# The first dense matrix in seven products: a change to an attention, experts and dense kernel

## The chip, the cores and the metric

The kernel is one program on one core of a Trainium2 chip. The metric is the device time of one execution in microseconds, as the median of several runs. Five engines work side by side and are tied by semaphores only: PE multiplies matrices into PSUM, whose eight banks hold 512 float32 columns each on 128 partitions; DVE and ACT do elementwise work and empty PSUM; POOL issues the indirect transfers and does a little elementwise work; SP issues the other transfers. Each engine takes its instructions strictly in the order of the program, so an instruction that waits holds back all that stands behind it on its engine.

## The reference, cut to what matters

```python
def reference(q, k, v, moe_w_gate, moe_w1, moe_w2, moe2_w_in, moe2_w_out):
    x = retention(q, k, v)              # per head: (q k^T / 8 * decay) v; 4608 tokens x 512
    logits = x @ moe_w_gate             # 8 experts
    e = argmax(logits); gate = softmax(logits)[e]
    y = gate * (max(x @ w1[e], 0) @ w2[e])      # 512 -> 1024 -> 512, one expert per token
    h = y @ moe2_w_in                   # 512 -> 2048
    r = max(h, 0); g = r * r
    return g @ moe2_w_out               # 2048 -> 512
```

The gate is positive and the last two layers are a square and a matrix after it, so a gate on the rows of y is the same as its square on the rows of the output.

## The kernel before

Precision first, since it sets the count of the matmuls: every operand is held as a high part (`F32R`) and the rest (`lo`), and a product is three matmuls, high·high, high·low, low·high.

The program has three stages. **Attention** takes 36 tiles of 128 tokens and writes x to `x_d` in DRAM. **The experts** run in a loop over 64 units `u` (expert `e = u // 8`, slice `f = u % 8` of 128 hidden features). A unit multiplies 640 gathered tokens: `first(u + 1)` is 24 matmuls of 320 columns in two halves, each into one of three banks `l1_ps`; ACT writes the high part `hh` and DVE the rest `hl` of each half (L718, L719), after which the bank is free; `second(u)` is 15 matmuls of 512 columns (L736 to L738). So PE takes `first(u + 1)` before `second(u)`, and the second half of the next unit's `first` wants the bank of this unit's first half. Beside that a unit splits the weights of a later unit (`split_unit`, L97 and L98, on DVE, for one unit in eight on POOL), turns the next expert's tokens (`transp`, L684 to L689, for f of 2 to 6) and, for 32 of the units, changes 512 columns of the dense weights, which come as the two 32-bit words of a float64, into a high and a low part (`split_wide`, L119 to L147: seven DVE operations, two on ACT), which SP writes to `wd_d` in DRAM. At u = 18 stands `rest_of` (L757 on, the branch at L759), a branch (`tc.If`) for tokens beyond an expert's 640 places; with this input it is not taken, but every engine passes it. The last six units hold back their `second`, which then runs token tile by token tile, so that `finish` (gate times accumulator, scattered to `y_d`) frees the first rows early.

**The dense stage** has 9 blocks of 512 tokens and 16 slices of 128 hidden features. All 16 slices of both weight matrices stay on the chip as 16 tiles of 1 MB (pools `w_a`, `w_b`, `w_c`, `w_d`), loaded once. `up(b, f)` (L937) is 12 matmuls of 512 columns, `squares` is relu on ACT, square on DVE, high part on ACT and rest on DVE, `down(b, f)` (L958 to L960) 12 matmuls into four accumulator banks. For the first block the first four slices run in halves of 256 columns, since the rows of its last two tiles arrive late. The order is written by hand: `up` runs two steps ahead of `down`, and block b + 1 is fetched from `y_d` and turned during block b.

Of the kernel before, what the change touches and what calls it, by code (L numbers as in the profile page):

```python
# [19 lines left out]
NT = 36  # L20
# [7 lines left out]
REST = 18  # L28
# [3 lines left out]
GROUPS = [(0, 8), (8, 16), (16, 24), (24, 30), (30, 36)]  # L32

# [4 lines left out]
def body(ctx, tc, att, tab_v, tab_x, masks, wg, ident, pick, cst, wu, wd, out):  # L38
# [9 lines left out]
    w_a = scope(ctx, "w_a", 4)  # L48
    pools = {}
    early = ctx.enter_context(ExitStack())  # L50
    places = scope(early, "places", 1, side="right")
# [4 lines left out]
    wd_d = dram.tile([NF, 128, 2, 1024], F32, name="wd_d")  # L56
    x_d = dram.tile([NTOK, 512], F32, name="x_d")
    l_d = dram.tile([NTOK, NE], F32, name="l_d")
# [3 lines left out]
    cf = const.tile([128, C_N], F32, name="cf")  # L62
    ub = places.tile([128, 128], BF16, name="ub")
    sel = places.tile([128, 4, 128], F32, name="sel")
    ones = places.tile([128, 128], BF16, name="ones")
    rk = places.tile([128, NT], I32, name="rk")
    inv = places.tile([128, 2 * NS], F32, name="inv")
# [22 lines left out]
    def load_unit(u, on=None):  # L90
        raw = (on or pools["stg"]).tile([128, 1024], F32, tag="raw", name="raw")
        sp.dma_start(out=raw, in_=wu[u])
        return raw

    def split_unit(u, raw, on):
        w = ring(u).tile([128, 2, 1024], F32R, tag="w", name="w")
        act.activation(out=w[:, 0], in_=raw, func=AF.Copy)  # L97
        on.tensor_tensor(out=w[:, 1], in0=raw, in1=w[:, 0].bitcast(F32), op=ALU.subtract)  # L98
        return w
# [11 lines left out]
    def load_wide(j):  # L111
        raw = pools["cr_p"].tile([128, 512, 2], I32, tag="craw", name="craw")
        v, s = divmod(j, 2)
# [5 lines left out]
    def split_wide(j, raw):  # L119
        v, s = divmod(j, 2)  # L120
        low, high = raw[:, :, 0], raw[:, :, 1]
        m = pools["cv_p"].tile([128, 512], F32, tag="cm", name="cm")
        x = pools["cv_p"].tile([128, 512], F32, tag="cx", name="cx")
        t = pools["cv_p"].tile([128, 512], I32, tag="ct", name="ct")
        a = pools["cv_p"].tile([128, 512], F32, tag="ca", name="ca")
# [9 lines left out]
            out=a.bitcast(I32), in0=xi, scalar=-0x40000000, in1=t, op0=ALU.bitwise_and, op1=ALU.bitwise_or  # L135
        )
        vec.tensor_scalar(
            out=m.bitcast(I32), in0=a.bitcast(I32), scalar1=-0x800000, scalar2=None, op0=ALU.bitwise_and
        )
        vec.scalar_tensor_tensor(  # L140
            out=x, in0=low.bitcast(U32), scalar=2.0 ** -52, in1=m, op0=ALU.mult, op1=ALU.mult
        )
        w = pools["cw_p"].tile([128, 2, 512], F32R, tag="cw", name="cw")
        act.activation(out=w[:, 0], in_=a, func=AF.Copy)
        vec.tensor_tensor(out=a, in0=a, in1=w[:, 0].bitcast(F32), op=ALU.subtract)
        vec.tensor_tensor(out=w[:, 1], in0=a, in1=x, op=ALU.add)
        return lambda: sp.dma_start(out=wd_d[v, :, :, 512 * s:512 * s + 512], in_=w.bitcast(F32))  # L147

    def load_dense(v, wpool):
        w = wpool.tile([128, 2, 1024], F32R, tag="w", name="w")  # L150
        sp.dma_start(out=w.bitcast(F32), in_=wd_d[v])
        w_q[NE * 8 + v] = w
# [57 lines left out]
    def fetch_logits(sm, index, n):  # L210
        lg = sm.tile([128, n, NE], F32, tag="lg", name="glg")
        for i in range(n):
            fetch_rows(lg[:, i], l_d[:, :], index[:, i:i + 1])
        return lg

# [17 lines left out]
    def gate_of(sm, lg, n):  # L233
        mx = sm.tile([128, n], F32, tag="mx", name="gmx")
        vec.tensor_reduce(out=mx, in_=lg, axis=AX.X, op=ALU.max)
        vec.tensor_tensor(out=lg, in0=lg, in1=mx.unsqueeze(2).to_broadcast([128, n, NE]), op=ALU.subtract)
        act.activation(out=lg, in_=lg, func=AF.Exp)
        vec.tensor_reduce(out=mx, in_=lg, axis=AX.X, op=ALU.add)
        vec.tensor_scalar(out=mx, in0=mx, scalar1=1e-9, scalar2=None, op0=ALU.add)
        g = sm.tile([128, n], F32, tag="g", name="gg")  # L240
        vec.reciprocal(out=g, in_=mx)
        return g

    w_q = {}

# [6 lines left out]
    with ExitStack() as es:  # L252
# [14 lines left out]
        lgt = rt.tile([128, NT, NE], F32, name="lgt")  # L267
# [143 lines left out]
        def group(t0, t1):  # L411
# [3 lines left out]
            def one():  # L415
                lg = lgt[:, t0:t1]
                late.append(
                    lambda: sp.dma_start(
                        out=l_d[128 * t0:128 * t1, :].rearrange("(t p) e -> p t e", p=128), in_=lg
                    )  # L420
                )
# [84 lines left out]
        def lead_rows():  # L506
# [5 lines left out]
            for i in range(LEAD):  # L512
                row = pools["cv_p"].tile([128, 512], F32, tag=("cm", "cx")[i], name="lead")
                fetch_rows(row, x_d[0:128 * GROUPS[2][1], :], lead_idx[:, i:i + 1])
                lead_s.append(row)

        def lead_turn(i):
            ps = sc_ps.tile([128, 4, 128], F32, tag="sc", name="turn")
            turn_rows(ps, lead_s[i])
# [5 lines left out]
        raw = {}  # L525
        lead_x = [
            pools["cw_p"].tile([128, 2, 512], F32R, tag="cw", name=f"lead{s}").rearrange(
                "p s (k n) -> p (s k) n", n=128 * LEAD
            ) for s in range(2)
# [30 lines left out]
        for t in range(NT):  # L560
# [39 lines left out]
            if t % 6 == 2 and 12 <= t < 36:  # L600
                w_q[t // 6 - 2] = split_unit(t // 6 - 2, raw.pop(t - 2), pool)
# [4 lines left out]
        for v, tags in ((4, ("ct", "ca")), (5, ("cm", "cx"))):  # L606
            halves[v] = [pools["cv_p"].tile([128, 512], F32, tag=t, name="half") for t in tags]
# [4 lines left out]
    pools["w_b"] = scope(ctx, "w_b", 4, reuse="tile")  # L612
    xs_p = scope(ctx, "xs_p", 1, reuse="tile")
    xf_p = scope(ctx, "xf_p", 2, reuse="tile")
# [3 lines left out]
    yi, yt = {}, {}  # L618
# [4 lines left out]


    def fetch(b, t0=0, t1=4):
        if t0 == 0:
            yi[b] = xs_p.tile([128, CT, 4, 128], F32, tag="xs", name="yi")
            yt[b] = columns()
        y = yi[b].rearrange("q t a c -> q (t a) c")
        rows = y_d[512 * b:512 * b + 512, :].rearrange("(t i) (a c) -> a i t c", i=32, a=4)  # L630
        ts = slice(4 * t0, 4 * t1)
        for a in range(4):
            d = sp.dma_start(out=y[32 * a:32 * a + 32, ts], in_=rows[a][:, ts])  # L633
            if b < 2:
# [6 lines left out]
            if b == 0:  # L641
                read.append(d.ins)

    def turn(b, *tiles, chunks=(slice(0, 4),)):
        src = {i: xf_p.tile([128, 4, 128], F32, tag="xf", name="yf") for i in tiles}
        for ks in chunks:
            for i in tiles:
                vec.transpose(
                    out=src[i][:, ks].rearrange("f k (t i) -> f k t i", i=32),
                    in_=yi[b][:, i].rearrange("q t (k j) -> q k t j", k=4)[:, ks],  # L650
                )
        for ks in chunks:
# [438 lines left out]
```

## Time and profile before

| | |
|---|---|
| median of 3 runs | 1433.29 us (1427.59 to 1435.78) |
| the profiled execution | 1436.04 us, of which the span from first to last instruction 1434.2 us |
| PE busy | 1391.3 us (97%) |
| DVE, ACT, POOL busy | 712.5 us (50%), 435.3 us (30%), 313.2 us (22%) |
| granted PE clock, mean | 0.991 of full speed |
| moved by DMA | 172.51 MB, mean 120 GB/s |

Busy is the time in which at least one instruction of the engine ran, so overlapping matmuls count once. The stages, by the slices of the page: attention to about 200 us, experts to 644 us, dense to the end.

### The profile page before, as it was taken

Reading aid. Unit: us, or ns where it says so; the run is one execution under the profiler, and the core shown is the slowest. Engines: PE = TensorE matmul, PEld = TensorE weight load, DVE = VectorE, ACT = ScalarE, POOL = GpSimd, SP = SyncE. Lnnn points to the kernel's source line nnn. Section 1 sums busy time; section 2 is a strip of 40 time slices with the busy share of each in tenths; the row PEclk is TensorE's granted clock in tenths of the full one; section 3 lists DMA queues with packets and bytes.
Section 4 is the critical chain, followed back from the end, with each engine's and each line's share of the span. In section 5 each row is a group of like instructions: output and inputs, shape, how many; then the busy total and the mean of one; then the engine's idle time right before and its main releaser. Section 6 shows DMA issues by size and latency. Waiting matters only on the chain.

```text
span 1434.2 us, 20323 instructions
## 1 busy us (share of the span) xinstructions
PE 1391.3 (97%) x8217; PEld 1192.2 (83%) x8217; DVE 712.5 (50%) x1187; ACT 435.3 (30%) x764; POOL 313.2 (22%) x277
## 2 busy tenths in 40 slices
PE   7989799998999999999999999999999999999998
PEld 5777688887999999998888888888888888888887
DVE  5667656886888888723323233232333323333222
ACT  1212233443444444422222222222222222222221
POOL 2223246765657557310000000000000000000000
PEclk9999999999999999999999999999999999999999
DMA  8999744765756757538120020200102020020000
GB/s 309 293 298 303 210 131 135 241 226 176 234 186 222 227 185 237 189 134 312 81 59 0 1 59 0 59 1 27 33 0 59 1 57 3 0 59 1 30 0 30
DMA packets 92406, 172.51 MB, mean 120 GB/s; under 512 B 16654, under 2 KB 54030, under 8 KB 86672
## 3 DMA queue, kind: packets, MB, share of 16 engines
q1 hardware_dynamic: 82944, 151.03, 33.3%
q0 software_dynamic: 9360, 20.10, 4.3%
q8 instruction: 66, 1.08, 0.3%
q14 instruction: 36, 0.29, 0.1%
HBM read 125.86 MB, written 46.28 MB: 120 GB/s over the span
## 4 chain that ended last, share of the span: by engine, by line
PE 72%; issue 3%; DMA 1%; POOL 0%; SPq 0%; ACT 0%; POOLq 0%; DVE 0%
PE fl L937 27%; PE fa L959 9%; PE fa L958 9%; PE fa L960 9%; PE l L712 3%; PE l L713 3%; PE l L714 3%; PE acc L737 3%; PE acc L736 3%; PE acc L738 3%; DMA w<-wd_d 1%; DMA y_d<-y,sidx 0%; POOL y_d L227 0%; SPq L633 0%; DMA yi<-y_d 0%
## 5 line engine op out<-in xcount | busy, mean ns | idle before, releaser
L937 PE MATMUL fl<-xt,w 128*128 128x512 f32 (+1 forms) x1776 | 415.3, 383 | 1.5 <-DMA w<-wd_d 1.5
L937 PEld LDWEIGHTS fl<-xt,w 128*128 128x128 f32 x1776 | 327.1, 188 | 67.3 <-issue 1.9
L944 DVE TENSOR_TENSOR fr<-fr 128x512 f32<-128x512 f32 x144 | 99.8, 693 | 401.2 <-ACT fr L942 401.2
L958 PE MATMUL fa<-w,gh 128*128 128x512 f32 x576 | 224.1, 389 | 0.0
L959 PE MATMUL fa<-w,gh 128*128 128x512 f32 x576 | 224.1, 389 | 0.0
L960 PE MATMUL fa<-w,gl 128*128 128x512 f32 x576 | 224.1, 389 | 0.0
L942 ACT ACTIVATE fr<-fl 128x512 f32<-128x512 f32 x144 | 86.2, 599 | 416.0 <-PE fl L937 416.0
L206 POOL DMA_INDIRECT xs<-x_d,qidx x140 | 154.0, 1100 | 44.4 <-issue 42.4
L712 PE MATMUL l<-xt,w 128*128 128x320 f32 (+1 forms) x480 | 150.2, 313 | 8.8 <-DVEq L759 6.2
L713 PE MATMUL l<-xt,w 128*128 128x320 f32 (+1 forms) x480 | 149.8, 312 | 0.0
L948 DVE TENSOR_TENSOR gl<-fr,gh 128x512 fp32r<-128x512 f32 x144 | 99.8, 693 | 100.6 <-ACT gh L946 100.6
L714 PE MATMUL l<-xt,w 128*128 128x320 f32 (+1 forms) x480 | 149.7, 312 | 0.0
L958 PEld LDWEIGHTS fa<-w,gh 128*128 128x128 f32 x576 | 108.1, 188 | 22.5
L959 PEld LDWEIGHTS fa<-w,gh 128*128 128x128 f32 x576 | 108.2, 188 | 22.3
L960 PEld LDWEIGHTS fa<-w,gl 128*128 128x128 f32 x576 | 108.0, 188 | 22.4
L736 PE MATMUL acc<-w,hh 128*128 128x512 f32 x320 | 125.7, 393 | 0.0
L737 PE MATMUL acc<-w,hh 128*128 128x512 f32 x320 | 125.3, 392 | 0.0
L738 PE MATMUL acc<-w,hl 128*128 128x512 f32 x320 | 124.8, 390 | 0.1
L946 ACT ACTIVATE gh<-fr 128x512 fp32r<-128x512 f32 x144 | 91.0, 632 | 109.7 <-DVE fr L944 109.7
L712 PEld LDWEIGHTS l<-xt,w 128*128 128x128 f32 x480 | 90.7, 189 | 12.1 <-issue 6.6
L713 PEld LDWEIGHTS l<-xt,w 128*128 128x128 f32 x480 | 90.7, 189 | 2.4 <-DVE xt L689 0.2
L714 PEld LDWEIGHTS l<-xt,w 128*128 128x128 f32 x480 | 90.7, 189 | 0.0
(140 smaller groups left out, 1511.4 us busy)
## 6 DMA issues: line engine op xcount, KB each, us to landing
raw<-wu SPq DMA_DIRECT2D x62, 512.0 KB, 4.0
in<-att SPq DMA_DIRECT2D x28, 1024.0 KB, 7.9
craw<-wd SPq DMA_DIRECT2D x32, 512.0 KB, 5.6
wd_d<-cw SPq DMA_DIRECT2D x32, 512.0 KB, 6.7
w<-wd_d SPq DMA_DIRECT2D x16, 1024.0 KB, 16.4
x_d<-xr SPq DMA_DIRECT2D x144, 64.0 KB, 5.4
yi<-y_d SPq DMA_DIRECT2D x32, 256.0 KB, 6.0
out<-fo SPq DMA_DIRECT2D x32, 256.0 KB, 2.8
```

What stands on the lines that cost most here:

```text
L206: pool.indirect_dma_start(out=xs, out_offset=None, in_=src, in_offset=bass.IndirectOffsetOnAxis(ap=index, axis=0),)
L712: pe.matmul(ps, w[:, 0, k], hi[:, k, cs], start=(k == 0), stop=False)
L713: pe.matmul(ps, w[:, 0, k], lo[:, k, cs], start=False, stop=False)
L714: pe.matmul(ps, w[:, 1, k], hi[:, k, cs], start=False, stop=(k == 3))
L736: pe.matmul(acc[i], hh[:, cs], w[:, 0], start=(f == 0), stop=False)
L737: pe.matmul(acc[i], hh[:, cs], w[:, 1], start=False, stop=False)
L738: pe.matmul(acc[i], hl[:, cs], w[:, 0], start=False, stop=(f == 7))
L937: pe.matmul(ps, w[:, s, k], x[:, k, ts], start=(n == 0), stop=(n == 11))
L944: vec.tensor_tensor(out=gg, in0=r, in1=r, op=ALU.mult)
L958: pe.matmul(acc[i], gh[:, cs], w[:, 0], start=(f == 0), stop=False)
L959: pe.matmul(acc[i], gh[:, cs], w[:, 1], start=False, stop=False)
L960: pe.matmul(acc[i], gl[:, cs], w[:, 0], start=False, stop=(f == 15))
```

## The change

**The dense matrix `w_in`** is multiplied by Strassen's scheme. The weights of two hidden slices and both halves of the 512 features are four blocks (`LEFT`), two groups of tokens and the same halves of the features four others (`RIGHT`); seven products of sums of blocks take the place of eight. A product is 2 chunks of the features times 3 parts, 6 matmuls. Tokens come as block 0 alone (T = 0, two groups of 256, 256 columns a matmul) and then four pairs of blocks (T = 1 to 4, 512 columns). For each of 8 slice pairs `j` the products run in the order 5, 1, 4, 7, 3, 2, 6; some accumulate in the same bank (4 then 2; 5, 3, 6; 1 then 7), and ACT and DVE combine the rest (`keep`, `block`). All hidden blocks of T are kept in SBUF (`g`), and `down` follows after all of T's `up`, for T of 1 to 4 one block `h` after the other.

**The weights no longer stay.** 14 tiles of 1 MB of product factors and 8 of `w_out` lie in `ws_d`, and each T streams them through a ring of four tiles (`stream`, pool `w_a`): 22 tiles for T = 0, 30 for each other T. A tile's place is filled again as soon as its last product is done. The first eight tiles have places of their own.

**The factors are made in the expert loop**, units 5 to 52, one job a unit, in groups of six: two `narrow` (the float64 words to float32), two `left_factors` (sums of blocks, high and low parts), two `split_wide` for `w_out`. A job has three steps: before the unit's `first`, after it, and at the head of the next unit. The pool `cw_p` of the results has one buffer where it had two, and `cv_p` one of three planes.

**The rest.** `rest_of` stands after unit 63 instead of unit 18. The gates are worked out once at unit 57, and their squares scale the output in `store`; `finish` copies only; the logits are no longer stored and fetched. `split_unit` runs on POOL for two units in eight, and the subtractions of `split_unit` and `transp` are issued later than their copies.

```diff
-    pools["cw_p"] = scope(early, "cw_p", 2, side="right")
+    pools["cw_p"] = scope(early, "cw_p", 1, side="right")
...
+    def narrow(raw, tag, made):
+        t, m, x = words(raw)
+        yield
+        low_word(raw, m, x)
+        a = pools["cv_p"].tile([128, 512], F32, tag=tag, name=tag)
+        vec.tensor_tensor(out=a, in0=t, in1=x, op=ALU.add)
+        made.append(a)
+        yield
+        yield
+    def split_wide(v, raw):
+        t, m, x = words(raw)
+        yield
+        w = pools["cw_p"].tile([128, 4, 512], F32R, tag="cw", name="cw")[:, 0:2]
+        act.activation(out=w[:, 0], in_=t, func=AF.Copy)
+        low_word(raw, m, x)
+        yield
+        vec.tensor_tensor(out=t, in0=t, in1=w[:, 0].bitcast(F32), op=ALU.subtract)
+        vec.tensor_tensor(out=w[:, 1], in0=t, in1=x, op=ALU.add)
+        yield lambda: sp.dma_start(
+            out=ws_d[14 + v // 2, :, 2 * (v % 2):2 * (v % 2) + 2], in_=w.bitcast(F32)
+        )
+    def left_factors(j, x0, x1, part):
...
+        yield
+        sums = pools["cv_p"].tile([128, 3, 512], F32, tag="cv", name="sums").rearrange("p a (b n) -> p (a b) n", n=256)
+        w = pools["cw_p"].tile([128, 4, 512], F32R, tag="cw", name="cw").rearrange("p k (s n) -> p k s n", s=2)
+        s = blk[LEFT[these[-1] - 1][1]]
+        act.activation(out=w[:, n - 1, 0], in_=s, func=AF.Copy)
+        for m, i in enumerate(these[:-1]):
+            _, a, op, b = LEFT[i - 1]
+            vec.tensor_tensor(out=sums[:, m], in0=blk[a], in1=blk[b], op=op)
+        act.activation(out=w[:, 0:n - 1, 0], in_=sums[:, 0:n - 1], func=AF.Copy)
+        yield
+        vec.tensor_tensor(out=w[:, n - 1, 1], in0=s, in1=w[:, n - 1, 0].bitcast(F32), op=ALU.subtract)
+        vec.tensor_tensor(
+            out=w[:, 0:n - 1, 1], in0=sums[:, 0:n - 1], in1=w[:, 0:n - 1, 0].bitcast(F32), op=ALU.subtract
+        )
...
+    def stream(on):
+        n = len(ring_q)
+        w = on.tile([128, 4, 2, 256], F32R, tag="w", name="wq")
+        sp.dma_start(out=w.rearrange("p k s n -> p k (s n)").bitcast(F32), in_=ws_d[stream_of[n]])
+        ring_q.append(w)
...
         for u in range(NU):
...
+            if last_job:
+                f_ = next(last_job)
+                if f_:
+                    f_()
+                last_job = None
...
+            if job:
+                next(job)
+            for f_ in rests[1:]:
+                f_()
             if u + 1 < NU:
                 first(u + 1, (1,) if u + 1 < MORE else (0, 1))
...
+            if job:
+                next(job)
+                last_job = job
             if u < NU - FIN:
                 second(u, range(LEAD if u < MORE else 0, CT))
-                if u == REST:
-                    rest_of()
                 if f == 7:
                     finish(e)
+        rest_of()
+        for _ in range(2):
+            stream(w_a)
...
+        def up(T, j, i, n):
+            k = 7 * j + KEPT.index(i)
+            p = bank_of[i]
...
+            terms = [(c, a, b) for c in range(2) for a, b in ((0, 0), (0, 1), (1, 0))]
+            for m, (c, a, b) in enumerate(terms):
+                pe.matmul(
+                    ps, w[:, a, c], xc[T][i, b][c], start=(i in (5, 1, 4) and m == 0), stop=(m == 5),
+                    skip_group_check=True,
+                )
...
+            def block(b, ps, s):
+                o = g[b][:, j, 0:n]
+                if s is None:
+                    act.activation(out=o, in_=ps, func=AF.Relu)
+                    act.activation(out=o, in_=o, func=AF.Square)
+                else:
+                    vec.tensor_tensor(out=o, in0=ps, in1=s, op=ALU.add)
+                    vec.scalar_tensor_tensor(out=o, in0=o, scalar=0.0, in1=o, op0=ALU.max, op1=ALU.mult)
...
+        head = [(0, "up", j, i) for i, j in (
+            (4, 0), (4, 1), (4, 2), (2, 0), (2, 1), (2, 2), (4, 3), (2, 3),
+            (5, 0), (5, 1), (1, 0), (1, 1), (7, 0), (7, 1), (3, 0), (3, 1), (6, 0), (6, 1),
+        )]
+        slots = []
+        for T in range(5):
+            slots += [(T, "up", j, i) for j in range(8) for i in ORDER if (T, "up", j, i) not in head]
+            slots += [(T, "down", h, f) for h in range(2 if T else 1) for f in range(16)]
...
+        for n in range(2):
+            stream(w_a)
+        for T, _, j, i in head[:8]:
+            up(T, j, i, 256)
...
+            t = tile_of(T, what, a, b)
+            left[t] -= 1
+            if left[t] == 0 and t >= 4 and t + 4 < len(stream_of):
+                stream(w_a)
```

## Rows read from the trace of the kernel before

**Rows 1.** Busy time by stretch: stretch, its length, busy per engine, clock, DMA share, GB/s.
```profile
300.00:340.00 40.00, 33.82 (x186) 30.90 (x185) 27.07 (x44) 15.20 (x26) 26.60 (x25) 0.91 0.72 236
340.00:580.00 240.00, 240.00 (x1349) 218.83 (x1348) 199.65 (x328) 107.72 (x186) 146.76 (x130) 1.00 0.64 209
...
664.00:1424.00 760.00, 760.00 (x3354) 629.50 (x3353) 244.98 (x359) 200.16 (x328) 0.00 (x0) 1.00 0.12 35
```

**Rows 2.** Groups by line and form, PE: operands, shape, count, busy us, mean ns.
```profile
L937 PE MATMUL fl<-xt,w 128*128 128x512 f32 x1680 | 403.6, 389 | 1.5 <-DMA w<-wd_d 1.5
...
L937 PE MATMUL fl<-xt,w 128*128 128x256 f32 x96 | 11.7, 283 | 0.0
```

**Rows 3.** Timeline of PE at the start of the dense stage: start, length, line, shape, count.
```profile
644.35 7.83 PE L937 MATMUL fl<-xt,w 128*128 128x256 f32 x64
```

**Rows 4.** What PE waited for over the whole span: us in total, times, longest.
```profile
PE l L712 <- DVE hl L719: 2.6, 3, 1.1
...
PE fl L937 <- DMA w<-wd_d: 1.5, 1, 1.5
```

**Rows 5.** The branch at unit 18: timeline of PE, its sequencer's branch, the chain.
```profile
324.68 0.40 PE L737 MATMUL acc<-w,hh 128*128 128x512 f32 x1
...
327.65 0.39 PE L738 MATMUL acc<-w,hl 128*128 128x512 f32 x1
334.21 0.61 PE L712 MATMUL l<-xt,w 128*128 128x320 f32 x1 [6.18 <-DVEq L759]
...
L759 PEldq COMPARE_BRANCH  x1: 3632/3632/3632, 324.6 to 324.6; - x1
...
339.58 0.23 PE acc L737
346.52 0.23 PE acc L737
```

**Rows 6.** Groups by form on DVE; the first four from 340 to 580 us.
```profile
L98 DVE TENSOR_TENSOR w<-raw,w 128x1024 fp32r<-128x1024 f32 x30 | 36.6, 1220 | 6.9 <-ACT w L97 6.4
L719 DVE SCALAR_TENSOR_TENSOR hl<-l,hh 128x320 fp32r<-128x320 f32 x69 | 31.5, 483 | 10.7 <-ACT hh L718 10.7
...
L127 DVE SCALAR_TENSOR_TENSOR cx<-cm,craw 128x512 f32<-128x512 f32 x22 | 15.2, 689 | 0.8
...
L131 DVE TENSOR_SCALAR ct<-cx 128x512 int32<-128x512 int32 x22 | 9.4, 427 | 0.8
...
L656 DVE TENSOR_TENSOR xt<-yf,xt 128x256 fp32r<-128x256 f32 x2 | 0.8, 422 | 0.2 <-ACT xt L655 0.2
```

**Rows 7.** SP's timeline, and landing of wd_d<-cw: 340 to 580 us, then 590 to 610.
```profile
346.55 0.38 SPq L114 DMA_DIRECT2D craw<-wd  x1
346.98 0.53 SPq L147 DMA_DIRECT2D wd_d<-cw  x1
...
DMA to landing us min/median/max: 4.9/6.7/7.9
...
601.66 0.52 SPq L147 DMA_DIRECT2D wd_d<-cw  x1
...
DMA to landing us min/median/max: 3.1/4.8/6.6
```

**Rows 8.** The chain at the dense stage's start, and all landings of w<-wd_d (1 MB).
```profile
644.71 0.30 SPq L633
...
646.01 2.02 DMA yi<-y_d
...
DMA to landing us min/median/max: 4.7/16.4/21.2
```

**Rows 9.** The output's transfers from the page, and two groups by form on ACT.
```profile
out<-fo SPq DMA_DIRECT2D x32, 256.0 KB, 2.8
...
L718 ACT ACTIVATE hh<-l 128x256 fp32r<-128x256 f32 x8 | 3.0, 379 | 12.2 <-PE l L714 12.2
...
L342 ACT ACT_TABLE_LOAD x1 | 1.3, 1283 | 1.6 <-DVE sts L553 1.6
```

More of the change, by code (lines that the diff above doesn't have):

```diff
@@ new lines, in body, with weights, keep @@
+        bank_ps = {"b1": b1_ps, "b4": b4_ps, "b5": b5_ps}
+        steps = [(None, 0)] + [(2 * n - 1, 2 * n) for n in range(1, 5)]
+        xc, cg, pt, acc = {}, {}, {}, {}
+        first_of = [0] + [22 + 30 * n for n in range(4)]
+        left = {}
+        def weights(n, k):
+            return ring_q[n][:, k]
+        sums, half, cut = {}, {}, set()
+        def keep(name, key, ps, n):
+            if n < 512 and key % 2 and (name, key - 1) in half:
+                s = half.pop((name, key - 1))[:, 256:512]
+            else:
+                s = s_p.tile([128, 512], F32, tag=name, name=name)
+                if n < 512:
+                    half[name, key] = s
+            sums[name, key] = s
+            act.activation(out=s[:, 0:n], in_=ps, func=AF.Copy)
@@ L954, in down @@
+        def down(T, h, f, tiles=range(4)):
+            hi, lo = cg[T, h, f]
+            w = ring_q[first_of[T] + 14 + 8 * h + f // 2][:, 2 * (f % 2):2 * (f % 2) + 2].rearrange("p k s n -> p k (s n)")
             for i in tiles:
@@ new lines, in body @@
+        x2.append(turn(yi[0][:, 3], s_p, "s5"))
+        first_of_them(order[3:], x0_t, x2)
+        for T, _, j, i in head[8:]:
+            up(T, j, i, 256)
+        jobs = []
+        for m, (T, what, a, b) in enumerate(slots):
+            if (T, what, a, b) == (0, "up", 3, 5):
+                late_es.close()
+                places_es.close()
+                pools["cg_p"] = scope(es, "cg_p", 3, reuse="tile")
+                xe_p = scope(es, "xe_p", 1, reuse="tile")
+            for s in slots[m + 2:m + 3] + (slots[m + 1:m + 2] if what == "up" else []):
+                if s[1] == "down" and (s[0], *s[2:]) not in cg:
+                    halve(s[0], *s[2:])
+            if what == "up":
+                up(T, a, b, 512 if T else 256)
+                if T < 4 and b == 6 and a in (4, 5):
+                    if a == 4:
+                        load, jobs = prepare(T + 1)
+                    load(a - 4)
+            elif m < len(slots) - 2:
+                if (a, b) == (0, 0) and T == 0:
+                    x_v.extend(places_of_factors())
+                down(T, a, b)
+                if b == 15:
+                    store(T, a)
+                for _ in range(2 if T else 3):
+                    if jobs:
+                        jobs.pop(0)()
+            t = tile_of(T, what, a, b)
+            left[t] -= 1
+            if left[t] == 0 and t >= 4 and t + 4 < len(stream_of):
+                stream(w_a)
```

478 lines of the change are left out of this document (279 added, 199 removed).

## The prediction

> **What bounds the kernel now.** I read the busy times by stretch first. From 340 to 580 us, in the expert loop, and from 664 to 1424 us, in the dense stage, PE is busy all of the time at the full clock, while DVE has 83% and 32% and the transfers 209 and 35 GB/s [rows 1]. So both stages are as long as their matmuls, and a matmul taken out is time taken out, as long as nothing else becomes late. The dense stage takes 760 us / 3354 = 0.2266 us per matmul of 512 columns [rows 1]. The second view is what PE waited for: after the attention stage there is little, 2.6 us for `hl`, 1.5 us for weights of the dense stage [rows 4], and one hole of another kind, the branch at unit 18 [rows 5]. The third is the price of a narrow matmul, as T = 0 will run at 256 columns: 64 of them in 7.83 us are 0.122 us each [rows 3], so half the columns cost 54% of the time, and no weight load holds them up.
>
> **The matmuls.** Before, `up` has 1680 of 512 columns and 96 of 256 [rows 2]: 1680 x 0.2266 + 96 x 0.122 = 392.4 us. After, a pass T is 8 pairs x 7 products x 6 = 336 matmuls: four passes of 512 columns are 1344 x 0.2266 = 304.5 us, T = 0 is 336 x 0.122 = 41.0 us, together 345.5 us. `down` keeps its 1728. The gain is 46.9 us, less than an eighth of 392 because of the 54%.
>
> **The branch.** At unit 18 PE ends at 328.0 and starts again at 334.21, waiting for DVE's own way through the branch, and then runs at the half clock: 0.91 granted over that 40 us stretch [rows 1, 5]. The second matmul of two neighbouring units' `second` lies 339.58 - 324.68 = 14.9 us apart where a unit takes 346.52 - 339.58 = 6.94 us [rows 5], so the branch costs 8.0 us. It waits for DVE since the next `first` takes a bank that the branch's body uses. After unit 63 the next PE work is the held-back `second`, which uses none of them. PE then has only its own passage, 3.63 us from 324.6, which ended at 328.3 with the matmuls ending at 328.0 [rows 5]. What is queued behind the branch: on ACT and DVE the copies of `finish`, the first one wanted 18 x 0.2266 = 4.1 us later; on POOL the scatters, but POOL has nothing to do for units before and passes early; on SP the weight streams. Bounds of the new cost: 0 and the old 8.0. I take 0.5, nearest to 328.3 against 328.0.
>
> **The factors in the expert loop.** DVE now has 199.65 / 240 x 6.94 = 5.77 us of work in a unit [rows 1, 5]. A `split_wide` is five operations of 0.69 and two of 0.43 [rows 6], 4.31 us; 22 of them in 34.6 units are 2.74 us a unit, which go; another 1.22 / 8 = 0.15 us goes to POOL [rows 6]. The six new jobs: two `narrow` of 3.62, two `split_wide` of 4.31, and two `left_factors` with sums of 256 columns at 0.42 and subtractions, 2.6 and 1.95 (768 columns estimated at 0.95, between 0.69 and 1.22 [rows 6]). That is 20.4 us in six units, 3.41 each, and DVE comes to 6.29 us of 6.94, 91%. It fits, but tightly. The deadline is the first half's `hl`: PE wants its bank 6.94 + 1.77 = 8.7 us into a unit. In the heaviest unit DVE first has a third step (1.4), a transpose (0.69), `split_unit` (1.22), four word operations (2.24) and a subtraction (0.69), 6.2 us; it can begin them about 1.5 us ahead of the unit, so `hl` is out near 5.2 and 3.5 us are spare. Fewer such units would be no loss, so nothing is gained here; I take 3 us for units that queue up, bounds 0 and the hand-overs below.
>
> **The hand-overs of the one `cw` buffer.** In each group of six, three results follow each other: the copy of the next job (ACT, second step) waits until the transfer of the last has landed. Behind that copy on ACT stand the next unit's copies and `hh`; PE waits for those. Three hand-overs take copies and third steps of about 2.3, 1.8 and 2.1 us, 6.2 together [rows 6, 9], and three landings; they have three units, 20.8 us, and the 3.5 us spare, 24.3. The landing of 512 KB is 3.1 us at the least, for the one issued alone at 601.66, and 6.7 us in the median, where SP issued it 0.43 us behind a read [rows 7]. Landings of 768 KB and 1 MB aren't in the trace as writes; 1 MB as a read is 4.7 us at the least [rows 8], so I add 0.8 and 1.6 us. Alone: 3.1 + 3.9 + 4.7 + 6.2 = 17.9, hidden. At the median: 6.7 + 7.5 + 8.3 + 6.2 = 28.7, over by 4.4 us a group, 35 us in eight groups. In the new order the reads of a unit are issued when the unit before has split its weights, some 4 us ahead of the transfer, so I take a value near the lone one, up to 5.2 us for 512 KB, where the overrun is nil.
>
> **The start of the dense stage.** The eight head products are 48 x 0.122 = 5.9 us. The seventh needs tile 6, whose place PE frees only in the last tail tile, and SP issues it behind the rows' fetches, done at 646.0 [rows 8]; with 4.7 us it is there at 650.7, and the product is due 36 x 0.122 = 4.4 us after 644.35, at 648.7 [rows 3, 8]. I take 2 us, bounds 0 and 8 (landings of several such tiles are longer [rows 8]).
>
> **The ring in T = 0.** A tile is asked for when the tile four before is done and wanted ten products later, 10 x 0.73 = 7.3 us; a lone tile lands in 4.7 us [rows 8]. I take 1 us, bounds 0 and 30 (six tiles at 12.3, a value between the least and the median of the old tiles, which were issued in rows of twelve). For T of 1 to 4 a tile has 13.6 us, and the need is 1 MB in 5.44 us, 193 GB/s, below what the expert loop moves [rows 1].
>
> **Between `down` of two blocks** the accumulators are stored with nothing between: three places for `o`, an output landing in 2.8 us [rows 9], four tiles, so the fourth copy waits. 0.5 us, four times: 2 us, bounds 0 and 6.
>
> **Hidden.** Combining products costs ACT and DVE seven operations each a pair, 4.9 us at 0.69 against 42 x 0.2266 = 9.5 us of PE; in T = 0 seven at about 0.4, 2.8 against 5.1 us [rows 6, 9]. If this cover went, a wait of 0.3 us at each of 40 pairs would be 12 us. The next pass's factors lie in `down`, 44 us or longer. The old wait for weights, 1.5 us [rows 4], goes, since the streams start before the tail.
>
> **The sum.** 1436.0 - 46.9 - 8.0 - 1.5 + 0.5 + 3 + 2 + 1 + 2 = 1388.1 us against the profiled execution's own time. That lies 2.7 us above the median shown, 1433.3, so the forecast for a median is 1386 us. With all unknown costs at nil it is 1377; with moderate ones, 1405.
>
> **The rivals.**
> (A) The hand-overs land as the median write did: 35 us in place of 3, 1418 us. For it: the only many-row price is 6.7 us [rows 7]. Against it: those transfers stood right behind a read. The Trainium skill speaks for this rival: "DMA: Bandwidth & Descriptors", section "Issuing engines are not separate DMA queues", says that transfers of all issuers run on the same 16 engines and interleave, so the gathers of POOL would lengthen a write that SP issues alone. By that rule the sum would be nearer 1418. The trace agrees as far as SP's own reads go, 6.7 us behind one against 3.1 alone [rows 7]; what a gather adds no row isolates.
> (B) Slower than before: the same buffer, landings beyond 7.3 us. There three hand-overs pass 24.3 by 6.3 us, which is the 50 us that all else gains, over eight groups. At 7.9, the longest between 340 and 580 us [rows 7], it is 64 us and 1447 us. Against it: that is the end of the old distribution, in worse company.
> (C) The ring starves T = 0, with the half clock behind the holes: 30 us, 1417 us. Against it: a lone tile takes 4.7.
> (D) ACT's new Square needs another table than Relu, and the pair switches both ways: a load is 1.28 us, and the run had one only, with Copy, Abs, Relu and Exp [rows 9]. Four loads a pair are 5.1 us; with 4.9 of work that is 10.0 against 9.5 for PE in 32 pairs, and 7.9 against 5.1 in 8: about 38 us, 1424 us. The Trainium skill, "ScalarE: Activation LUTs", section "Table sets: the hidden batching unit", says that cheap functions stand in every set and names relu, copy and abs, not square; by that rule at most one or two loads come, and the sum stays.
>
> **How the numbers follow.** Chances: forecast 0.70, A 0.12, B 0.08, C 0.07, D 0.03. The range of 8 in 10 runs from 1377 to 1420: it takes in the forecast's own 1377 to 1405 (nearly all of 0.70) and A and C at their prices. A measurement here can tell some 0.5%, 7 us, so faster means below 1426. All of the forecast, 0.10 of A and 0.04 of C and D are faster: 0.84. Same: 0.07, the rest of A, C and D. Slower: B and a remainder, 0.09.
>
> **What would show it.** Matmuls at 0.2266 and 0.122 us in the dense stage and 1344 + 336 of them for `up`; units of 6.94 us without a hole at 18; ACT's copy into `cw` waiting little for a landing in the units after `left_factors`, and PE's waits on `hl` below 5 us. A and B would show as PE idle before `first` in the last units of each group, with ACT waiting for `ws_d`. C would be PE waiting for `ws_d` between 620 and 700 us. I am wrong if PE in the dense stage waits for DVE or ACT at every pair.

## The result, and the profile of the changed kernel

| | before | after | best of the experiments (e7_factors_split) |
|---|---|---|---|
| median | 1434.53 us | 1452.55 us | 1405.24 us |
| ratio to the kernel before, 95% interval | | 1.0126 [1.0098, 1.0153] | 0.9786 [0.9758, 0.9815] |
| profiled execution, span | 1434.2 us | 1445.9 us | 1408.3 us |
| expert stage | 462.0 us | 484.9 us | 465.7 us |
| dense stage | 785.9 us | 785.1 us | 759.9 us |
| of it `up` of T = 0 | | 63.8 us | 57.5 us |

The change was forecast at 1386 us, faster; it is 1.3% slower, and outside the range. The two stages are read from the starts of the matmuls in the timelines: the expert stage from the first `first` to the first dense matmul, the dense stage from there to PE's end. The attention stage ahead of them took 172 to 182 us in the runs below, in no order of the edits, so the ledger leaves it out. Four of these runs (e1_pad_right, b1_pad, e2_s_first, e3_split_dve) fell into a stretch in which all kernels were slower, the kernel before at 1523 us, with idle time in the expert loop that the profile doesn't explain, so they are read by stage from their traces. By the prediction's own terms the expert stage should have been 462.0 - 8.0 + 0.5 + 3 = 457.5 us and the dense stage 785.9 - 46.9 - 1.5 + 2 + 1 + 2 = 742.5 us. Together 1200.0 was forecast and 1270.0 came: 70 us are to be found.

Busy time by stretch of the kernel after, columns as in [rows 1]:

```profile
340.00:580.00 240.00, 228.24 (x1249) 205.52 (x1248) 197.51 (x318) 102.74 (x182) 125.55 (x108) 0.99 0.66 222
740.00:1420.00 680.00, 677.58 (x2898) 544.06 (x2897) 313.01 (x535) 262.31 (x503) 54.26 (x70) 1.00 0.60 209
...
900.00:1000.00 100.00, 100.00 (x429) 80.40 (x428) 38.19 (x56) 35.07 (x57) 0.00 (x0) 1.00 0.59 201
```

Two things are to be seen. In the expert loop PE does 1249 matmuls where it did 1349 [rows 1], and is idle for 12 us. In the dense stage PE is busy all of the time at the full clock, and yet it does 429 matmuls in 100 us. The same 100 us of the kernel before:

```profile
900.00:1000.00 100.00, 100.00 (x443) 82.84 (x442) 32.17 (x48) 26.99 (x45) 0.00 (x0) 1.00 0.10 22
```

There it was 443. Busy time hides this: a matmul that takes 3% longer looks as busy as before.

What PE waited for in the kernel after (us in total, times, longest), for comparison with [rows 4]:

```profile
PE l L794 <- DVE hl L801: 22.1, 8, 8.5
...
PE b L1087 <- ACT s L1073: 8.4, 5, 6.5
PE b L1087 <- ACT xt L731: 4.0, 1, 4.0
...
PE fa L1149 <- DVE fo L1164: 1.7, 1, 1.7
PE fa L1149 <- DMA wq<-ws_d: 1.6, 1, 1.6
PE acc L818 <- PEq L840: 1.4, 1, 1.4
```

The first line was 2.6 us. The second and third are new and stand at the start of the dense stage. The branch is the last line: 1.4 us in place of the hole of 6.18 us in [rows 5].

The longest wait for `hl` is made here, on DVE and POOL (timeline: start, length, engine, line, operation, shape, count):

```profile
224.43 4.65 POOL L115 TENSOR_TENSOR w<-raw,w 128x1024 fp32r<-128x1024 f32 x2
224.78 4.86 DVE L142 SCALAR_TENSOR_TENSOR cv<-cv,craw 128x512 f32<-128x512 f32 x1 [1.24 <-ACT cv L141]
...
232.28 0.69 PE L794 MATMUL l<-xt,w 128*128 128x384 f32 x1 [8.51 <-DVE hl L801]
```

The first word operation of a job, 0.69 us [rows 6], takes 4.86 us: it starts 0.35 us behind two subtractions of `split_unit` in a row on POOL and ends 0.56 us behind their end. What stands behind it on DVE, `hl` included, comes late. From 190 to 640 us the instructions of DVE that exceed the median of their form by over 0.3 us add up to 23.5 us in 13 instructions; in the kernel before it was 9.9 us in 7. All 20 of them overlap a subtraction on POOL and end 0.28 to 0.56 us behind its end.

The start of the dense stage, timeline of POOL, ACT and PE:

```profile
660.58 0.98 POOL L284 DMA_INDIRECT y_d<-y,sidx  x1 [5.92 <-DMA yi<-y_d]
...
666.38 0.38 ACT L1073 ACTIVATE s<-b 128x256 f32<-128x256 f32 x1 [7.76 <-DMA y_d<-y,sidx]
...
656.63 3.70 PE L1087 MATMUL b<-xt,wq 128*128 128x256 f32 x30
666.82 2.93 PE L1087 MATMUL b<-xt,wq 128*128 128x256 f32 x12 [6.49 <-ACT s L1073]
670.22 1.65 PE L1087 MATMUL b<-xt,wq 128*128 128x256 f32 x6 [0.47 <-ACT s L1073]
675.87 1.47 PE L1087 MATMUL b<-xt,wq 128*128 128x256 f32 x4 [4.00 <-ACT xt L731]
```

ACT's third copy into `s4` waits 7.76 us for a scatter of `y`: the second buffer of `s4` lies where the last `y` lay, and that row scatter leaves POOL only when the fetches of the next rows have landed. The stretch from 656 to 676 us, with 9.04 us of PE work in 20, has a granted clock of 0.66, between PE's two levels: the matmuls of 256 columns after the first wait start 0.213 us apart, at 1.2 GHz, where those ahead of it took 0.118, at 2.4.

### The profile page after: what moved, and what is told of

Same layout as the page of the kernel before. It is cut to its first block, busy times and chain, and to the rows that moved or that the text cites. A ratio compares the mean times of both kernels' runs of the same rounds, so it can differ in the third digit from the quotient of the medians.

```text
span 1445.9 us, 21410 instructions
## 1 busy us (share of the span) xinstructions
PE 1380.7 (95%) x8121; PEld 1166.2 (81%) x8121; DVE 842.8 (58%) x1484; ACT 532.3 (37%) x1046; POOL 343.0 (24%) x324
## 4 chain that ended last, share of the span: by engine, by line
PE 58%; DMA 16%; DVE 10%; issue 8%; POOL 5%; ACT 3%; SPq 1%; DVEq 0%; POOLq 0%; ACTq 0%
PE b L1087 24%; PE fa L1151 9%; PE fa L1149 9%; PE fa L1150 9%; DMA in<-att 7%; POOL xs L269 3%; DMA ws_d<-cw 3%; DMA y_d<-y,sidx 2%; DMA xs<-x_d,qidx 1%; DMA wq<-ws_d 1%; DVE hl L801 1%; DVE cv L142 1%; POOL y_d L284 1%; PE l L794 1%; DVE cv L152 1%
## 5 line engine op out<-in xcount | busy, mean ns | idle before, releaser
L1087 PE MATMUL b<-xt,wq 128*128 128x512 f32 (+1 forms) x1296 | 276.4, 371 | 15.9 <-ACT s L1073 8.4
L1087 PEld LDWEIGHTS b<-xt,wq 128*128 128x128 f32 x1296 | 224.8, 192 | 62.4 <-ACT s L1073 9.5
L1149 PE MATMUL fa<-wq,ch 128*128 128x512 f32 x576 | 226.9, 394 | 4.0 <-DVE fo L1164 1.7
L1151 PE MATMUL fa<-wq,cl 128*128 128x512 f32 x576 | 229.2, 398 | 0.0
L1150 PE MATMUL fa<-wq,ch 128*128 128x512 f32 x576 | 226.8, 394 | 0.0
L1139 DVE TENSOR_TENSOR cl<-g,ch 128x512 fp32r<-128x512 f32 (+1 forms) x160 | 106.4, 674 | 188.2 <-ACT ch L1138 185.9
L794 PE MATMUL l<-xt,w 128*128 128x320 f32 (+1 forms) x480 | 152.2, 317 | 22.2 <-DVE hl L801 22.1
L1138 ACT ACTIVATE ch<-g 128x512 fp32r<-128x512 f32 (+1 forms) x160 | 91.0, 583 | 174.3 <-PE fa L1150 174.3
L1149 PEld LDWEIGHTS fa<-wq,ch 128*128 128x128 f32 x576 | 108.1, 188 | 30.7 <-ACT ch L1138 3.1
L1150 PEld LDWEIGHTS fa<-wq,ch 128*128 128x128 f32 x576 | 108.1, 188 | 27.5
L1151 PEld LDWEIGHTS fa<-wq,cl 128*128 128x128 f32 x576 | 108.1, 188 | 25.7 <-DVE cl L1139 0.3
L794 PEld LDWEIGHTS l<-xt,w 128*128 128x128 f32 x480 | 91.5, 191 | 27.4 <-DVE hl L801 24.8
L1087 PE MATMUL b<-xe,wq 128*128 128x512 f32 x384 | 95.1, 396 | 0.0
L795 PEld LDWEIGHTS l<-xt,w 128*128 128x128 f32 x480 | 91.7, 191 | 2.6 <-DVE xt L771 0.2
```

Source lines behind the costliest of these rows:

```text
L794: pe.matmul(ps, w[:, 0, k], hi[:, k, cs], start=(k == 0), stop=False)
L795: pe.matmul(ps, w[:, 0, k], lo[:, k, cs], start=False, stop=False)
L1087: pe.matmul(ps, w[:, a, c], xc[T][i, b][c], start=(i in (5, 1, 4) and m == 0), stop=(m == 5), skip_group_check=True,)
L1139: vec.tensor_tensor(out=lo[:, o], in0=s, in1=hi[:, o].bitcast(F32), op=ALU.subtract)
L1149: pe.matmul(acc[i], hi[:, cs], w[:, 0], start=(f == 0), stop=False)
L1150: pe.matmul(acc[i], hi[:, cs], w[:, 1], start=False, stop=False)
```

## The experiments

Three theories for the 70 us: (1) the place of a matmul's operands in SBUF sets the interval of 0.233 us (100 us / 429); (2) reused memory holds up T = 0; (3) POOL's `split_unit` holds DVE.

### The place of the operands

In the kernel before, by the program's memory plan, both operands of every matmul of 512 columns in the expert and dense stages begin a multiple of 512 bytes apart. In the changed kernel `w_a` went to the right side, and it stands 352 bytes off that grid from `xt`, `h`, `ch`, `cl` and `xe`.

**e1_pad_right**
```diff
+    scope(ctx, "pad", 1, side="right").tile([128, 8], F32, name="pad")
     w_a = scope(ctx, "w_a", 4, side="right")
```


> The changed kernel with 32 bytes of padding in each partition ahead of the ring w_a, which stays on the right side of SBUF; its four tiles then begin at a multiple of 64 bytes, like the factors and h that they are multiplied with, where in the changed kernel they begin 32 bytes past one. Theory 1, the two operands of a matmul begin at different places within 64 bytes: the interval of the dense stage falls from 0.2333 to 0.2266 us (3072 x 6.7 ns = 21 us), half of the expert loop's 1960 matmuls likewise (6.6 us), so 24 to 28 us less, about 1426 us. Rival, the side itself or the stream of 1 MB tiles: the interval stays at 0.2333 and the time within 2 us of 1452.

Measured: the dense interval lies between 226 and 236 ns with a mean of 229 to 233 by stretch; 430 matmuls from 900 to 1000 us. The ratio, 0.9827 [0.9617, 1.0037] to the 1523 us, settles nothing. The expectation fails: a multiple of 64 bytes (here the distance is 320) isn't enough, or the place isn't the cause.

**b1_pad**, the converse in the kernel before:
```diff
     w_a = scope(ctx, "w_a", 4)
+    scope(ctx, "pad", 1).tile([128, 8], F32, name="pad")
```


> The kernel before with 32 bytes of padding in each partition behind the ring w_a on the left; w_a and w_d then stand 32 bytes past a multiple of 64, and all of xt, h, gh, gl, w_b and w_c on one. Theory 1: the dense products with f of 0 to 7 (w_d, w_a) go from 0.2266 to 0.2333 us, those with f of 8 to 15 stay; 3354 / 2 x 6.7 ns = 11 us, with half of the expert loop's matmuls 6.6 us more: 16 to 19 us slower than the kernel before. Rival, the side or the stream: within 2 us of the kernel before.

Measured: the dense stage goes from 785.9 to 796.4 us, 10.5 us where 11 were expected (a second kernel with the old places, b2_pool56 below, has 785.5). The whole kernel doesn't show it: its ratio to the 1523 us is 0.9899 [0.9826, 0.9972], where 16 to 19 us more were expected; its expert loop is among the disturbed ones. Two stretches of one block, the first with the weights of `w_d` and `w_a` (off the grid from the moving and stationary operands), the second with those of `w_b` and `w_c` (on it):

```profile
1070.00:1102.00 32.00, 32.00 (x139) 25.75 (x138) 9.88 (x15) 7.47 (x13) 0.00 (x0) 1.00 0.26 67
1115.00:1147.00 32.00, 32.00 (x143) 26.49 (x142) 10.21 (x15) 8.64 (x14) 0.00 (x0) 1.00 0.00 1
```

139 matmuls against 143 in 32 us. Sorted by the distance of their operands, the matmuls of 512 columns in the whole stage start 233 ns apart in the mean off the grid and 227 on it. The rows of the next block are fetched in the first kind of stretch only, but they are in the kernel before as well, at 226.7 ns. So the place is a cause, and by e1_pad_right a multiple of 64 bytes doesn't cure it. It is the distance and not the place of `w_a` by itself: by the memory plan the streamed weights begin 480 bytes past a multiple of 512 in the changed kernel, and so do all weights of the dense stage in the kernel before, where their partners begin there too.

**e1_pad352** and **e1_pad96**: as e1_pad_right, with `[128, 88]` and `[128, 24]` for the padding.

> The changed kernel with 352 bytes of padding ahead of the ring w_a on the right side: its tiles then lie a multiple of 512 bytes from the operands they meet, as all operands of the kernel before do, where 32 bytes had made it a multiple of 64 alone (and the dense interval stayed at 229 to 235 ns). Theory 1 in its second form, the distance of the two operands modulo 512 bytes: the dense stage's matmuls take 0.2266 us again, its length falls from 785 to 764 us, the expert loop's half of 1960 matmuls gives 6.6 us: 24 to 28 us in all, ratio to the kernel before 0.992 to 0.998 in place of 1.013. Rival, the right side itself: the interval stays at 0.230 to 0.234 and the ratio at 1.01.

> The changed kernel with 96 bytes of padding ahead of the ring w_a on the right side: its distance from the operands is then a multiple of 128 and 256 bytes, not of 512. If a multiple of 128 is enough, the dense interval is 0.2266 us and the time as with 352 bytes (ratio 0.999). If it takes 512 bytes, the interval stays at 0.230 to 0.234 us and the ratio at 1.008 to 1.013.

| | distance of w_a | matmuls from 900 to 1000 us | dense stage | ratio to before |
|---|---|---|---|---|
| after | 352 bytes | 429 | 785.1 us | 1.0126 [1.0098, 1.0153] |
| e1_pad_right | 320 | 430 | 779.9 us | 0.9827 [0.9617, 1.0037], to 1523 us |
| e1_pad96 | 256 | 443 | 767.6 us | 0.9975 [0.9957, 0.9994] |
| e1_pad352 | 0 (512) | 443 | 765.4 us | 0.9992 [0.9959, 1.0024] |

The stretch of e1_pad352 beside that of the kernel after:

```profile
900.00:1000.00 100.00, 100.00 (x443) 82.77 (x442) 40.66 (x60) 35.92 (x59) 0.51 (x1) 1.00 0.61 214
```

The same stream at 214 GB/s, the same side, the same program, and 443 matmuls. Theory 1 holds in its second form: at distances of 0 and 256 bytes modulo 512 the interval is 227 ns in the mean, at 320 and 352 it is 231 to 234. A smaller power of two that would do (128) wasn't tried, and the mechanism stays open. One expectation was too high: the expert loop gives nothing back (485.8 and 483.8 us against 484.9). It has little to give. In the changed kernel its matmuls of 512 columns with weights in `w_a`, 480 in all, start 233.6 ns apart in the mean and those on the grid 229.2, some 2 us together; its matmuls of 320 columns take 146 to 147 ns at every distance that occurs (0, 160, 256, 416 bytes), and those of 256 columns at the start of the dense stage take 117 to 120 on the grid and off it. PE's waits for `hl`, 23.7 us in both where it was 22.1, take up the 2 us.

### POOL's subtraction

**e3_split_dve**
```diff
-                rests.append(split_unit(v, raw.pop(v), pool if f in (5, 6) else vec))
+                rests.append(split_unit(v, raw.pop(v), vec))
```


> The changed kernel with no split_unit on POOL, all on DVE. Theory 3, POOL's 2.4 us subtraction holds DVE's instructions with two SBUF operands (0.69 becomes up to 4.9 us): DVE's long instructions go, PE's 22.1 us of waits for hl fall to under 8, and the time by 10 to 20 us, to about 1437. Rival, DVE is simply full (91% of a unit by the forecast, now 2 x 1.22 us more in eight units): the waits for hl stay or grow and the time is 1452 or more. A second rival, the one cw buffer makes ACT late: the waits stay at about 20 us with DVE's instructions at their short times.

Measured: PE's waits for `hl` are 2.5 us where e1_pad_right and e2_s_first have 9.4 and 7.8, and the expert stage is 515.2 us against 549.7 and 540.2; the ratio is 0.9876 [0.9731, 1.0022] to the 1523 us. The disturbed loop leaves no exact size; the next runs give it.

**e5_three**: e3_split_dve, `w_a` on the left (on the grid), and `s_p` ahead of `g_p` (below).

> The changed kernel with three edits: the ring w_a on the left side (a multiple of 512 bytes from h, xt, ch, cl and xe), s_p ahead of g_p, and every split_unit on DVE. The three theories together: dense interval 0.2266 (27 us with the expert loop's), the wait of 6.8 us at the start of T = 0 down to 2.5 (5 us), PE's waits for hl below 5 us (15 to 20 us): 45 to 52 us less than the changed kernel, ratio to the kernel before 0.975 to 0.982. Rival, the DVE that is now fuller gives the third back: 0.985 to 0.992. If the interval doesn't follow the place: 0.99 to 1.00.

Measured: 1408.88 us, ratio 0.9829 [0.9784, 0.9875], just above the first expectation's 0.982. Against e1_pad352, on the grid as well, the expert stage falls from 485.8 to 464.3 us: 21.5 us by the POOL edit, as `s_p` lies behind that stage and `w_a` is on the grid in both. DVE's excess, the sum named above, falls from 25.4 to 0.7 us.

**e8_pool6**: the last kernel below (e7_factors_split) with one of eight `split_unit` on POOL.
```diff
-                rests.append(split_unit(v, raw.pop(v), vec))
+                rests.append(split_unit(v, raw.pop(v), pool if f == 6 else vec))
```


> The kernel of the last run with one split_unit in eight units back on POOL (f = 6), as the kernel before has it and half of what the changed kernel has. Theory 3 (POOL's 2.4 us instruction holds DVE's with two SBUF operands): one or two DVE instructions in eight units get 1.2 to 2.4 us longer, PE's waits for hl rise from 8 us to 12 to 16, and the expert loop by 4 to 10 us, ratio 0.003 to 0.007 higher. Rival, DVE's own load is what counts: the waits fall with the 1.22 us in eight units taken from it, and the time falls by up to 5 us.

PE's wait for `hl` with none on POOL (e7_factors_split):

```profile
PE l L794 <- DVE hl L801: 7.7, 8, 3.7
```

and with one (e8_pool6):

```profile
PE l L794 <- DVE hl L801: 14.3, 9, 6.1
```

| `split_unit` on POOL in eight units | DVE's excess | PE's waits for `hl` | expert stage |
|---|---|---|---|
| 0 (e5_three, e6, e7) | 0 to 1.4 us | 7.6 to 8.5 us | 463.9 to 465.7 us |
| 1 (e8_pool6) | 9.0 us | 14.3 us | 472.4 us |
| 2 (after, e1_pad352, e1_pad96) | 23.5 to 25.4 us | 22.1 to 23.7 us | 483.8 to 485.8 us |

The first on POOL costs the stage 7 to 8 us and the second 11 to 13, though each takes 1.22 us off DVE every time [rows 6]. The rival, DVE's load, would have the opposite sign: DVE's own work is highest in the first line, and there the waits are least. In time e8_pool6 is at 0.9832 [0.9808, 0.9855] against 0.9786 [0.9758, 0.9815], which overlap a little; the stage and the waits carry the reading.

**b2_pool56**, the same dose in the kernel before:
```diff
-                w_q[v] = split_unit(v, raw.pop(v), pool if f == 6 else vec)
+                w_q[v] = split_unit(v, raw.pop(v), pool if f in (5, 6) else vec)
```


> The kernel before with a second split_unit in eight units on POOL (f = 5 and 6), as the change has it, and nothing else. The prediction took this for 0.15 us a unit off DVE and for nothing else. Theory 3: it costs even here, where DVE has 17% to spare: more DVE instructions of 2 to 5 us, PE's waits for hl from 2.6 to 4 to 10 us, the time 1 to 8 us more. Rival: DVE's spare time covers it, and the time is within 2 us of the kernel before or below.

Measured: 1.0014 [0.9996, 1.0033], 2 us that can't be told from none. The same long instructions come, here two subtractions on POOL and a word operation on DVE that the trace lets begin 0.34 us ahead of them and end 0.55 us behind them:

```profile
238.12 4.79 POOL L98 TENSOR_TENSOR w<-raw,w 128x1024 fp32r<-128x1024 f32 x2
...
237.78 5.68 DVE L127 SCALAR_TENSOR_TENSOR cx<-cm,craw 128x512 f32<-128x512 f32 x1
```

DVE's excess rises from 9.9 to 25.8 us, as much as in the changed kernel, but PE's waits only from 2.6 to 6.1 us. So the hold is the same in both kernels; what differs, by these waits, is the time that DVE has to make it good. The 20 us are of the two edits together: the second subtraction on POOL, and jobs that fill DVE.

### The start of the dense stage

**e2_s_first**
```diff
-        g_p = scope(es, "g_p", 1, reuse="tile")
         s_p = scope(es, "s_p", 2, reuse="tile")
+        g_p = scope(es, "g_p", 1, reuse="tile")
```


> The changed kernel with the two scopes s_p and g_p of the dense stage in the other order, so that s4, s5 and s1 take memory that is free at the start of T = 0 and the late block g22 the memory of the last y. Theory 2, the copies of the first products wait for the scatter of tile 4 through reused memory: the wait of ACT of 7.8 us at 658 to 666 us goes, T = 0 `up` falls from 63.8 to 47 to 50 us, the time by 13 to 18 us, to about 1437. Rival, the rows' fetches and the ring are late anyway (the seventh and eighth products, wq): the wait turns into one for those, gain under 5 us. Which block g lies over y decides whether a wait comes back later.

Measured: `up` of T = 0 falls from 63.8 to 59.1 us only (the whole kernel: 0.9902 [0.9837, 0.9966] to the 1523 us). The wait for the scatter goes, and the next ones step in: 2.21 us for the seventh tile `wq`, then the same 4.0 us for ACT's `xt` as before the edit. The rival is right. The 4.0 us are copies of the first pass's factors for tiles 2 and 3, which stand on ACT behind the copies of all eight head products.

**e6_factors_early**
```diff
-        for T, _, j, i in head[:8]:
+        for T, _, j, i in head[:4]:
...
-        for T, _, j, i in head[8:]:
+        for T, _, j, i in head[4:]:
```


> The kernel with the three edits, and the rest of the first pass's factors (tiles 2 and 3) made behind the fourth head product in place of the eighth, so that ACT's copies for them don't stand behind the copies of products 5 to 8. Theory: of the 4.4 us that PE waited for ACT's xt ahead of the ninth product 3 to 4 go, and 0.003 of the ratio beside the kernel with three edits. Rival, the rows of tile 3 come too late for it, or the copies hold back product 5 to 8: no difference or slower.

Measured: 0.9821 [0.9768, 0.9874], not to be told from e5_three; `up` of T = 0 61.2 to 57.2 us. The wait for `xt` is gone, but PE now waits for ACT's copy of product 7, which stands behind the factors:

```profile
PE b L1087 <- ACT s L1073: 6.3, 3, 5.3
PE b L1087 <- DMA wq<-ws_d: 3.4, 2, 2.4
```

**e7_factors_split**
```diff
-        first_of_them(order[3:], x0_t, x2)
-        for T, _, j, i in head[4:]:
+        first_of_them(order[3:4], x0_t, x2)
+        for T, _, j, i in head[4:8]:
+            up(T, j, i, 256)
+        first_of_them(order[4:], x0_t, x2)
+        for T, _, j, i in head[8:]:
             up(T, j, i, 256)
```


> The kernel with three edits, and the factors of tiles 2 and 3 in two parts: those of tile 2 and the first of tile 3 behind the fourth head product, the other six behind the eighth. With all ten behind the fourth, PE waited 5.3 us for ACT's copy of product 7 (4,3), which stood behind them. Theory: that wait falls to about 1 us, `up` of T = 0 from 57.2 to 53 us, the ratio to the kernel before by 0.002 to 0.004, to about 0.979. Rival, the chain of sums, copies and subtractions of tile 3 is the limit wherever its copies stand: PE waits the same time at the ninth product.

Measured: the ratio is as expected, 0.9786 [0.9758, 0.9815], but it can't be told from e5_three's 0.9829 [0.9784, 0.9875], and the mechanism isn't the expected one. `up` of T = 0 is 57.5 us in its profile (55.2 in that of e8_pool6, which has the same head):

```profile
644.32 4.55 PE L1087 MATMUL b<-xt,wq 128*128 128x256 f32 x36
652.15 1.65 PE L1087 MATMUL b<-xt,wq 128*128 128x256 f32 x6 [3.28 <-DMA wq<-ws_d]
654.27 5.60 PE L1087 MATMUL b<-xt,wq 128*128 128x256 f32 x30 [0.47 <-ACT s L1073]
661.72 0.50 PE L1087 MATMUL b<-xt,wq 128*128 128x256 f32 x2 [1.85 <-ACT s L1073]
```

The wait for ACT's `s` fell from 5.3 to 0.47 and 1.85 us, as expected; the transfers of `wq` took it, 6.8 us in two waits against 3.4. What PE waits for most at T = 0 now is the ring, and its waits differ from run to run. Beyond that it isn't settled.

### The branch

**e4_branch57**
```diff
                 if f == 7:
                     finish(e)
-        rest_of()
+                if u == NU - FIN - 1:
+                    rest_of()
```


> The changed kernel with the leftover branch one place earlier: behind the `second` of unit 57, the last pass of the loop that has one, so that six more `first` follow it, and not behind unit 63 ahead of the held-back `second`. Theory, as forecast: the next `first` takes a PSUM buffer that the branch's body uses and so waits for DVE's passage: a hole of 5 to 7 us with the half clock behind it, 6 to 9 us in all. Rival: PE passes in 1.4 us there as well, and the place is worth nothing, within 2 us.

Measured: 1.0162 [1.01, 1.0225], not to be told from 1.0126 by the time, where 6 to 9 us were expected. By the trace: the expert stage is 494.3 us against 484.9, but 4.4 us of that arise ahead of the branch, where the edit changes nothing. The last 260 matmuls ahead of the dense stage take 54.6 us in place of 49.6, and PE waits at the branch for another engine again, here for ACT's sequencer:

```profile
PE l L794 <- ACTq L840: 4.1, 1, 4.1
```

So the place behind the loop is worth 5.0 us beside this one inside it, in one trace of each.

## Why the prediction was wrong, step by step

**The matmuls, -46.9 us.** The counts were right (for `up` 1344 of 512 columns and 336 of 256 in place of 1680 and 96). The price failed: "four passes of 512 columns are 1344 x 0.2266" took an interval measured at one placing of the operands for a property of the shape. `down` was costed at nothing for the same reason. After T = 0's `up` the stage took 721.3 us; on the grid it takes 701.4 (e1_pad352) and 702.6 (e1_pad96), against 3072 x 0.2266 + 2 = 698. The whole dense stage lost 17.5 to 19.7 us by it (785.1 against 767.6 and 765.4). The full diff shows that `w_a` moves to the other side, and the prediction passed over the line. The 0.122 us for 256 columns held: 30 in 3.70 us.

**The factors in the expert loop, +3 us.** The step that failed is "another 1.22 / 8 = 0.15 us goes to POOL", booked as a gain. In the table above this second move costs 11 to 13 us, and the first, which the kernel before has too and bears at little cost, another 7 to 8 with the new jobs on DVE. [Rows 6] had DVE's mean times and not its longest ones, where the kernel before shows it already (9.9 us in 7 instructions). The Trainium skill has the rule: "SBUF — State Buffer", section "Who interferes with whom", says that a DVE instruction with two SBUF inputs contends with a GpSimd instruction that reads SBUF, and the loser blocks for the whole instruction. The trace agrees, 4.86 us against 0.69. Without the hold 7.6 to 8.5 us of waits are left, and only 2 to 3 of them are the queue that the 3 us stood for, in waits of 0.3 to 0.4 us, nearly all with DVE busy through the 8 us ahead. One of 3.5 to 4.0 us comes each time near the start of the loop, after DVE has stood 2.6 to 2.9 us for gathered rows (`xs`), and one of 1.6 to 2.0 us near 440 us. So the 3 us held for what it named; the price of POOL did not.

**The hand-overs, nil.** Right, and with them the case against rivals A and B. The landings of `ws_d<-cw` have a median of 3.8 us, inside the "up to 5.2":

```profile
ws_d<-cw SPq DMA_DIRECT2D x24, 512.0 KB, 3.8
```

ACT waited 19.4 and 19.2 us for them in the changed kernel, and 26.1 and 20.5 in e7_factors_split, whose expert stage is 19 us shorter. In both kernels ACT has ended its `hh` 2.2 us or more before DVE begins the `hl` that PE waits for, so it is DVE that is late and not ACT: hidden, but for the wait near 440 us, ahead of which in e5_three DVE stands 3.1 us for ACT's copy into `cw`. The landings of 768 KB and 1 MB have medians of 4.3 and 4.7 us, against 3.9 and 4.7 for the lone case. The time came out near B's 1447 us, by other causes.

**The start of T = 0, +2 and +1 us.** Forecast 41.0 + 3 = 44, measured 63.8. The named terms are near: the seventh tile costs 2.2 to 3.3 us where it shows, the ring 1 to 5. What failed stands under "Hidden": the prediction costed the combining of products once under way, and not that at the start ACT has copies of products, scattered rows' memory and ten copies of factors in one queue. The waits of 6.5 and 4.0 us and the half clock are that. Undoing them brought 63.8 to between 55 and 58.

**The branch, -8.0 + 0.5 us.** The mechanism is right: the hole at unit 18 is gone (200 matmuls around it take 36.1 us where they took 43.7), and PE waits 1.4 us at the new place where 0.5 was forecast. The 5.0 us of e4_branch57 are for another place, unit 57; unit 18 in the changed kernel wasn't tried.

**Stores, +2 us; old weights' wait, -1.5 us.** The first is right in size, 1.7 us for `fo`, though in one wait and not in four. The second isn't: the old wait is gone, and one of 1.6 us for `wq` stands at the first `down` of T = 0 (720.4 us). **Rival D** has no case; the page's groups show the one table load as before, with Square in use:

```profile
L413 ACT ACT_TABLE_LOAD x1 | 1.3, 1283 | 1.6 <-DVE sts L619 1.6
```

**The sum** is off by little: 1388.1 - 2.7 is 1385.4, written as 1386, and C's price gives 1386 - 1 + 30 = 1415, written as 1417.

The ledger of the 70 us: operands' place 18 to 20, POOL's hold 20, T = 0 20, DVE's other delays and the branch 7, the rest of the dense stage 3. The first is shown by a padding alone, the second by e5_three against e1_pad352 and by the doses; of the third some 6 to 9 us are shown, the rest is waits named in the trace. With all three undone, e7_factors_split's two stages still take 1225.6 us against the 1200.0 forecast.

## What to carry to other kernels

Where PE is busy all of the time, compare matmuls per 100 us before and after, and when a pool moves, look at how far the two operands of a matmul of 512 columns lie apart: 0 and 256 bytes modulo 512 were fast here. Before giving DVE work to POOL, look for DVE's longest instructions and not their mean: a second subtraction on POOL cost about 2 us, not clear of the noise, in the kernel before, whose DVE had time to spare, and 11 to 13 us in the changed one. At the start of a stage, write down the whole queue of the engine that frees PE's banks, with the memory that its outputs reuse.

## What the runs showed of the hardware that was not expected

The interval of back-to-back matmuls of 512 columns, each with its own weight load, is 227 ns where the two operands lie 0 or 256 bytes apart modulo 512, and mostly 229 to 238 ns at 320, 352 or 480; the busy share and the granted clock don't show it. Matmuls of 320 and 256 columns didn't change with the distance (146 to 147 and 117 to 120 ns). The Trainium skill, "SBUF — State Buffer", section "Who interferes with whom", says that TensorE never waits on another engine. A padding alone changes the interval here; whether another engine has a part in it no run shows. Two POOL subtractions in a row hold one DVE instruction for both of their lengths (4.65 and 4.86 us; 4.79 and 5.68). The hold isn't limited to instructions with two inputs in SBUF: three of the 13 long ones in the changed kernel are a `TENSOR_SCALAR` with one, 0.43 us otherwise, as here beside POOL:

```profile
281.43 2.48 POOL L115 TENSOR_TENSOR w<-raw,w 128x1024 fp32r<-128x1024 f32 x1 [0.99 <-ACT w L113]
281.69 2.50 DVE L152 TENSOR_SCALAR cv<-cv 128x512 int32<-128x512 int32 x1
```
